# Attention and a two-layer FFN on one core: small vector operations with fewer SBUF operands, scale products on POOL, weights rebuilt through PSUM, and their scale from a Gram matrix

## The chip, the cores and the metric

The kernel runs on 1 core of one Trainium2 chip. The metric is the device time of one launch in microseconds (us); before the change its median is 1268.44 us over 3 runs (1267.27 to 1268.83). The core has five engines with their own instruction queues: PE multiplies matrices (its weight loads are listed as PEld), DVE is the vector engine, ACT the engine for activations, POOL the general-purpose engine, and SP only issues DMA transfers here. SBUF is the working memory, PSUM the memory that PE writes its products to; POOL has no operand in PSUM anywhere in this kernel.

## What is computed

Per batch and head (8 batches, 8 heads, 576 tokens, head dimension 64), attention drops every score that is more than tau (0.02) below its row's maximum:

```python
scores = scale * np.matmul(q, k.transpose(0, 1, 3, 2))
thresh = np.max(scores, axis=-1, keepdims=True) - tau
scores = np.where(scores >= thresh, scores, -1000000000.0)
attn = softmax(scores)
x = np.matmul(attn, v)
h = x @ w_in
g = np.where(h >= 1, h, np.where(h <= -1, 0.0, (h + 1) ** 2 / 4))
out = g @ w_out
```

The softmax has 1e-09 added to its denominator; x holds the heads side by side, 4608 tokens of 512; w_in is 512 x 2048 and w_out 2048 x 512. The q, k and v come in f32, laid out with the head dimension first; the two weights come in f64.

## The kernel before

**Numbers.** Every matrix product is made of f16 parts: an operand is scaled by a power of two, rounded to f16 (the high part), and the remainder is rounded to f16 again (the low part). A product of two such operands takes three matmuls or a doubled contraction. The power of two comes from the data: sums of squares are formed on PE (`sums`), and `pow2` (lines 226 to 228) turns them into scales with bit operations on DVE.

**Weights.** `add_w` treats each weight in 16 units of 128 x 512. The f64 words are loaded into a staging buffer as pairs of u32 (line 436; for w_in the place is the still unused part of the w_out tile `WO`, 8 slots; for w_out it is the ring `x`, 5 slots, which later holds the FFN's input). ACT rescales the upper words (line 444), and three DVE operations put the bits of an f32 together in `WI` or `WO` (lines 448, 452, 456: shift; or with the shifted lower word; or with the sign). Their first operand reads every second u32. ACT then squares the unit with an accumulator (line 460); one matmul with ones adds the 16 sums up (line 478), and a chain of small DVE operations (lines 482 to 488) makes the weight's scales `wsc`. Odd units are then normed on POOL (498), rounded on ACT (501), and their remainder is formed on POOL (504); even units are normed and rounded on ACT (511), with the remainder on DVE (514).

**q, k and v.** For each pair of heads (`add_qk`) ACT sums the squares of q and k into a tile `pc` of 40 columns, PE adds them up over partitions (301), DVE makes scales: `pow2` on 6 columns (226 to 228), a product with tau's constants (308), and two products of 3 columns (316, 317) for the softmax. POOL norms q and k (324), ACT rounds (327), POOL forms the remainder (331), and 8 DMAs lay the parts out in `qq` and `kk`. V is handled alike for each batch (`add_v`; remainder on DVE, 396; a DMA transpose into `vst`).

**Tiles.** A pair's 2 x 576 query rows make 9 tiles of 128 rows by 576 keys, 288 in all. In `add_tile` PE forms the scores (595) into one of two PSUM buffers; DVE takes the row maximum (606) and from it, with the pair's constants, the bias of exp and the threshold (607: two columns at once, from two SBUF operands and a scalar per partition); ACT takes exp (610); DVE applies the mask and sums (614) and forms the reciprocal (618, 619); POOL scales (622), ACT rounds (625), POOL forms the remainder (628), and a DMA transposes the two parts into `eT` (631). After the last tile of a half pair PE multiplies with V (668), ACT and DVE cut the result into the FFN's input `x` (676, 680).

**FFN.** For each 128 tokens and each 512 of the 2048 hidden columns: 48 matmuls (729), Relu and square on ACT (735, 738), the gate on DVE (742), f16 parts on ACT and DVE (746, 750), 12 matmuls into the only accumulator `acc` (756). After four such steps ACT scales the accumulator (785) and a DMA stores it.

**The order.** Nothing is scheduled by hand at the place where it is written. Each step is a `plan.op` with an engine, an assumed duration, a key (roughly the number of the tile at whose time it is due) and its dependencies; `Plan.order` plays the whole kernel through and writes down which step each engine starts next, the one with the lowest key among those that are ready and whose buffers are free. The instructions are then emitted in that order, and each engine keeps its own order on the chip whatever the real durations are. Keys: tile j has key j; w_in's unit u has 0.7u - 2, w_out's 12 + 0.7u; the FFN lags the tiles that feed it by `LEAD` = 8. PSUM has the pools `s` (2, scores), `ph` (3, everything else) and `acc` (1).

Of the kernel before, what the change touches and what calls it, by code (L numbers as in the profile page):

```python
# [32 lines left out]
class Op:  # L33
    def __init__(self, eng, cost, key, fn, work):
        self.eng, self.cost, self.key, self.fn, self.work = eng, cost, key, fn, work
        self.take, self.uses, self.next, self.behind, self.left = [], [], [], [], 0


class Plan:


    HOP, TO_PE, LAND = 0.25, 0.6, 2.2
# [29 lines left out]
    def order(self):  # L72
# [6 lines left out]
        now = 0.0  # L79
        while True:  # L80
            woke = False
            for e, q in ready.items():
                if not idle[e]:
                    continue
# [57 lines left out]
def attn_ffn_kernel(ctx: ExitStack, tc: tile.TileContext, qT, kT, vT, tau, w_in, w_out, out):  # L142
# [68 lines left out]
    wssq = {w: cp.tile([P, NU], F32, name=f"ssq_{w}") for w in WT}  # L211
# [19 lines left out]
    def consts():  # L231
# [47 lines left out]
    def add_qk(b, p, need):  # L279
# [12 lines left out]
        def ssq(buf, n):  # L292
            return lambda: A.activation(junk, ap(buf, raw), AF.Square, accum_out=ap(cb, pc)[:, n : n + 1])
# [11 lines left out]
        def scales():  # L305
            c = ap(cb, pc)
            pow2(stat(sb.slot, 6), c[:, 2:8], c[:, 8:14], c[:, 14:20])
            V.tensor_tensor(c[:, 20:22], c[:, 18:20], tcs[:, 0:2], ALU.mult)  # L308

        def scales2():  # L310
            c = ap(cb, pc)
            u = c[:, 8:14].rearrange("p (v t) -> p v t", t=2)
            x = c[:, 14:20].rearrange("p (v t) -> p v t", t=2)
            k1 = c[:, 24:30].rearrange("p (v t) -> p v t", t=2)
            k2 = c[:, 30:36].rearrange("p (v t) -> p v t", t=2)
            V.scalar_tensor_tensor(k1[:, :, 0], u[:, :, 0], 2.0 ** 102 * D ** -0.5, u[:, :, 1], ALU.mult, ALU.mult)
            V.scalar_tensor_tensor(k2[:, :, 1], x[:, :, 0], tcs[:, 2:3], x[:, :, 1], ALU.mult, ALU.mult)

        sc1 = plan.op("DVE", 0.6, key - 3, scales, [ps, t_op], uses=[cb, sb])
        sc2 = plan.op("DVE", 0.3, key - 2, scales2, [sc1], uses=[cb])  # L320
        done = []
        for n, (rb, nb, ld) in enumerate(((rq, nq, lq), (rk, nk, lk))):
            def norm(rb=rb, n=n):
                G.tensor_scalar(ap(rb, raw), ap(rb, raw), ap(cb, pc)[:, 20 + n : 21 + n], 1.0, ALU.mult, ALU.mult)  # L324
# [31 lines left out]
    def add_v(b, need):  # L356
# [17 lines left out]
        def sums():  # L374
            T.matmul(stat(sb.slot, NPAIR), ones, rows_bf16(vssq[:, b, :]), start=True, stop=True)
# [35 lines left out]
    def add_w(w, keys):  # L411
        stats, bits = [], []
        for u in range(NU):
            key = keys(u)
            sb = plan.buf("wst" if w == "i" else "x")
# [30 lines left out]
            def b1(stage=stage, dsu=dsu):  # L446
                if F64:
                    V.tensor_scalar(dsu, stage()[:, :, 1], 3, None, ALU.logical_shift_left)

            def b2(stage=stage, dsu=dsu):  # L450
                if F64:
                    V.scalar_tensor_tensor(dsu, stage()[:, :, 0], 29, dsu, ALU.logical_shift_right, ALU.bitwise_or)

            def b3(stage=stage, dsu=dsu):
                if F64:
                    V.scalar_tensor_tensor(dsu, stage()[:, :, 1], 1 << 31, dsu, ALU.bitwise_and, ALU.bitwise_or)
# [372 lines left out]
```

## Time and profile before

| | |
|---|---|
| median of 3 runs | 1268.44 us (1267.27 to 1268.83) |
| the profiled execution | 1266.92 us, of which the span from first to last instruction is 1265.0 us |
| mean granted PE clock | 0.958 |
| busy PE, DVE | 1079.4 us (85%), 1071.6 us (85%) |
| busy ACT, POOL | 891.7 us (70%), 801.6 us (63%) |
| DMA | 184.53 MB, mean 146 GB/s |

A row of the groups of instructions reads: line, engine, operation, what is written from what, shapes, count, then busy us and mean ns of one, then the idle time of the engine just before them and what ended it. A row of the timeline reads: start, length, engine, line, operation. An engine can start its next instruction slightly before the profile ends the last one, so the distance between two starts can be smaller than the length. A row of waits reads: who waited for whom, us in total, times, longest. Line numbers are those of the kernel before, unless it is said otherwise.

### The profile page before, as it was taken

To read this page: it belongs to the slowest core of one execution; us is meant where nothing else is said; L and a number is where in the kernel's file an instruction comes from. 1 tells how busy PE (TensorE), PEld (TensorE's weight loads), DVE (VectorE), ACT (ScalarE), POOL (GpSimd) and SP (SyncE) were. 2 spreads that over 40 slices of the span, in tenths; PEclk is the share of its full clock that TensorE was granted. 3 is DMA by queue.
4 is the path that set the end of the run, shared out by engine and by line. 5 is a ranking of instruction groups with operands and counts; after the bars stand their busy time and mean duration, and the time that the engine had idled before them with its cause. 6 is when DMAs were issued, how large, how long until landed. Compare 5 with 4: busy or idle time off the path is not lost.

```text
span 1265.0 us, 31411 instructions
## 1 busy us (share of the span) xinstructions
PE 1079.4 (85%) x11818; PEld 784.4 (62%) x11818; DVE 1071.6 (85%) x2613; ACT 891.7 (70%) x1558; POOL 801.6 (63%) x791
## 2 busy tenths in 40 slices
PE   0124388899889998999989988999989999999998
PEld 0112365576657766776657766677677776777675
DVE  6999999889887889988897999888897988988532
ACT  6676677686668777877676767867687767777544
POOL 3688488855685667666674667765685667655300
PEclk9966699899989999999999999999999999999999
DMA  9985746975698669965698568965788579755400
GB/s 318 295 196 121 166 87 131 209 140 116 132 203 177 104 108 184 209 129 109 132 204 157 104 108 194 201 127 103 157 200 162 92 124 179 149 104 99 78 10 18
DMA packets 443816, 184.53 MB, mean 146 GB/s; under 512 B 406288, under 2 KB 414480, under 8 KB 443664
## 3 DMA queue, kind: packets, MB, share of 16 engines
q1 hardware_dynamic: 443664, 182.52, 70.9%
q8 instruction: 93, 1.52, 0.5%
q14 instruction: 59, 0.48, 0.1%
HBM read 45.09 MB, written 9.44 MB: 43 GB/s over the span
## 4 chain that ended last, share of the span: by engine, by line
DVE 42%; PE 38%; ACT 6%; issue 6%; DMA 4%; POOL 3%; SPq 0%; ACTq 0%; DVEq 0%; POOLq 0%
PE acc L756 15%; PE ph L729 14%; DVE sm L606 9%; DVE sm L607 8%; DVE e L614 7%; PE s L595 5%; PE ph L668 4%; DVE ph L742 3%; DVE g L750 3%; ACT e L610 2%; DVE vb L396 2%; POOL e L622 1%; DMA WO<-in_moe_w_in_dram 1%; DVE sm L619 1%; DVE x L680 1%
## 5 line engine op out<-in xcount | busy, mean ns | idle before, releaser
L628 POOL TENSOR_TENSOR hl<-e,hl 128x576 f16<-128x576 f32 x288 | 372.2, 1297 | 115.0 <-ACT hl L625 110.1
L729 PE MATMUL ph<-x,WI 128*128 128x128 f16 x6912 | 413.4, 221 | 10.1 <-DVE x L680 6.7
L729 PEld LDWEIGHTS <-WI 128*128 128x128 f16 x6912 | 402.4, 99 | 26.9 <-issue 13.1
L756 PE MATMUL acc<-WO,g 128*128 128x512 f16 x1728 | 400.1, 381 | 13.3 <-DVE g L750 12.2
L622 POOL TENSOR_SCALAR e<-e,sm 128x576 f32<-128x576 f32 x288 | 226.5, 792 | 210.4 <-DVE sm L618 119.0
L610 ACT ACTIVATE e<-s,sm,pc 128x576 f32<-128x576 f32 x288 | 237.7, 828 | 153.6 <-DVE sm L607 109.6
L756 PEld LDWEIGHTS <-g 128*128 128x128 f16 x1728 | 164.6, 98 | 202.3 <-DVE g L750 20.1
L595 PE MATMUL s<-kk,qq 128*128 128x288 f16 (+1 forms) x1280 | 190.4, 300 | 97.8 <-DVE e L614 79.1
L625 ACT ACTIVATE hl<-e 128x576 f16<-128x576 f32 x288 | 194.6, 678 | 77.6 <-POOL e L622 76.2
L614 DVE SCALAR_TENSOR_TENSOR e<-s,sm,e 128x576 f32<-128x576 f32 x288 | 229.4, 810 | 21.0 <-ACT e L610 18.4
L606 DVE TENSOR_REDUCE sm<-s 128x1 f32<-128x576 f32 x288 | 215.2, 747 | 28.9 <-PE s L595 28.3
L595 PEld LDWEIGHTS <-qq 128*128 128x128 f16 (+1 forms) x1280 | 112.0, 103 | 163.7 <-issue 116.3
L607 DVE SCALAR_TENSOR_TENSOR sm<-pc,sm 128x2 f32<-128x2 f32 x288 | 166.2, 577 | 10.2
L742 DVE SCALAR_TENSOR_TENSOR ph<-ph,scs,asq 128x512 f32<-128x512 f32 (+1 forms) x160 | 111.6, 699 | 59.5 <-ACT asq L738 56.0
L735 ACT ACTIVATE asq<-ph,scs 128x512 f32<-128x512 f32 (+1 forms) x160 | 115.0, 730 | 43.2 <-PE ph L729 42.9
L668 PE MATMUL ph<-eT,vst 128*64 128x256 f16 (+1 forms) x1792 | 131.9, 302 | 6.6 <-DVE g L750 4.5
L750 DVE SCALAR_TENSOR_TENSOR g<-ph,scs,g 128x512 f16<-128x512 f32 (+1 forms) x160 | 108.6, 688 | 30.8 <-ACT g L746 30.8
L668 PEld LDWEIGHTS <-vst 128*64 128x64 f16 x1792 | 103.4, 116 | 36.5 <-issue 23.2
L746 ACT ACTIVATE g<-ph,scs 128x512 f16<-128x512 f32 (+1 forms) x160 | 100.4, 640 | 25.5 <-DVE ph L742 24.4
L331 POOL TENSOR_TENSOR nat<-raw,nat 128x576 f16<-128x576 f32 x64 | 85.4, 1338 | 15.6 <-ACT nat L327 15.2
L738 ACT ACTIVATE asq<-asq 128x512 f32<-128x512 f32 x144 | 90.1, 626 | 1.9
L324 POOL TENSOR_SCALAR raw<-raw,pc 128x576 f32<-128x576 f32 x64 | 48.1, 758 | 30.1 <-DVE pc L308 15.4
(99 smaller groups left out, 703.0 us busy)
## 6 DMA issues: line engine op xcount, KB each, us to landing
kk<-nat SPq DMA_DIRECT2D x128, 144.0 KB, 3.4
raw<-in_q_dram SPq DMA_DIRECT2D x32, 288.0 KB, 3.6
raw<-in_k_dram SPq DMA_DIRECT2D x32, 288.0 KB, 3.7
raw<-in_v_dram SPq DMA_DIRECT2D x32, 288.0 KB, 4.0
qq<-nat SPq DMA_DIRECT2D x128, 72.0 KB, 2.3
WO<-in_moe_w_in_dram SPq DMA_DIRECT2D x16, 512.0 KB, 8.1
x<-in_moe_w_out_dram SPq DMA_DIRECT2D x16, 512.0 KB, 4.3
out_dram<-o SPq DMA_DIRECT2D x32, 256.0 KB, 2.6
```

The lines of the kernel that those rows point to most:

```text
L595: T.matmul(ap(s, s_ps)[r, f, :SH], q[:, hd, c : c + n], k[:, hd, l, f * SH : (f + 1) * SH], start=l == 0, stop=l == 1)
L606: V.tensor_reduce(t[:, 0:1], sv(), AX.XY, ALU.max, negate=True)
L607: V.scalar_tensor_tensor(t[:, 1:3], c[:, 24 + 2 * v : 26 + 2 * v], t[:, 0:1], c[:, 30 + 2 * v : 32 + 2 * v], ALU.mult, ALU.add)
L610: A.activation(halves(ap(e, es)), sv(), AF.Exp, bias=ap(m, sm)[:, 1:2], scale=ap(cb, pc)[:, 24 + 2 * v : 25 + 2 * v])
L614: V.scalar_tensor_tensor(halves(ap(e, es)), sv(), t[:, 2:3], halves(ap(e, es)), ALU.is_ge, ALU.mult, accum_out=t[:, 3:4])
L622: G.tensor_scalar(ap(e, es), ap(e, es), ap(m, sm)[:, 5:6], 1.0, ALU.mult, ALU.mult)
L625: A.activation(ap(x, hl)[:, :S], ap(e, es), AF.Copy)
L628: G.tensor_tensor(ap(x, hl)[:, S:], ap(e, es), ap(x, hl)[:, :S], ALU.subtract)
L668: T.matmul(o[hd * D : (hd + 1) * D, :n], vt[:, k, hd * D : (hd + 1) * D], t[:, kb, hd * n : (hd + 1) * n], start=k == 0, stop=k == NVB - 1)
L729: T.matmul(h[:, i], WTh["i"][:, u, wl * 512 + c * P : wl * 512 + (c + 1) * P], x[:, cc, xl, c0 : c0 + P], start=m == 0, stop=m == 3 * NCC - 1)
L742: V.scalar_tensor_tensor(hv()[:, :, c], hv()[:, :, c], scs[:, b, 0:1], tv()[:, :, c], ALU.max, ALU.min)
L756: T.matmul(ap(ab, accs), gv()[:, i, gl], WTh["o"][:, fc + i, wl * 512 : (wl + 1) * 512], start=fc + i == 0 and m == 0, stop=fc + i == NFC ...
```

## The change

It has five parts.

1. *The tile's threshold*: the operation at line 607 becomes two operations of one column, each with one SBUF tensor, a scalar per partition and a constant. The two-column constants in `pc` become single columns; filling them with zeros and minus ones at the start is left out.
2. *The pair's scales*: `pc` holds every value in the first of two columns, so that `pow2` reads and writes with a stride of two; the three products (308, 316, 317) leave DVE and become five POOL operations, in two steps of the plan.
3. *The weights' bits*: the first two of the three DVE operations write a PSUM buffer of the pool `ph`, and the second and third read it back. The sum of squares on ACT goes. In its place PE multiplies each unit, taken as the upper halves of its f32 words (bf16), with its own transpose, and adds all units up in `acc`: a Gram matrix of 128 x 128, whose largest element in each row replaces the sum.
4. *The weights' split*: all units take the former odd units' way, with the norm on ACT in place of POOL and the remainder on POOL; none has its remainder on DVE.
5. *The order*: w_out is staged in two of the five slots of `x` until its last unit's bits are done; its keys become 10 + 0.5u; the first batch's V is due 4 tiles later; no fifth FFN step starts before w_out's last unit's bits; the planner lets SP issue nothing while more than 3 us of transfers are outstanding; several assumed durations change.

The core of the diff:

```diff
+                if e == "SP" and dma > now + self.QUEUE:
+                    if wake <= now:
+                        wake = dma - self.QUEUE + 1e-6
+                        heapq.heappush(events, (wake, -1, 3, e, None))
                     continue
...
+    plan.free["x"], plan.free["wso"] = [0, 1, 2], [3, 4]
-    pc = ring("pc", 6, [40], F32)
+    pc = ring("pc", 6, [36, 2], F32)
...
         def scales():
-            c = ap(cb, pc)
+            c = ap(cb, pc)[:, :, 0]
             pow2(stat(sb.slot, 6), c[:, 2:8], c[:, 8:14], c[:, 14:20])
-            V.tensor_tensor(c[:, 20:22], c[:, 18:20], tcs[:, 0:2], ALU.mult)
         def scales2():
+            c = ap(cb, pc)[:, :, 0]
+            G.tensor_tensor(c[:, 20:22], c[:, 18:20], tcs[:, 0:2], ALU.mult)
+        def scales3():
-            V.scalar_tensor_tensor(k1[:, :, 0], u[:, :, 0], 2.0 ** 102 * D ** -0.5, u[:, :, 1], ALU.mult, ALU.mult)
-            V.scalar_tensor_tensor(k2[:, :, 1], x[:, :, 0], tcs[:, 2:3], x[:, :, 1], ALU.mult, ALU.mult)
+            G.tensor_scalar(c[:, 24:27], u[:, :, 0], 2.0 ** 102 * D ** -0.5, 1.0, ALU.mult, ALU.mult)
+            G.tensor_scalar(c[:, 27:30], x[:, :, 0], tcs[:, 2:3], 1.0, ALU.mult, ALU.mult)
+            G.tensor_tensor(c[:, 24:27], c[:, 24:27], u[:, :, 1], ALU.mult)
+            G.tensor_tensor(c[:, 27:30], c[:, 27:30], x[:, :, 1], ALU.mult)
...
-                    V.tensor_scalar(dsu, stage()[:, :, 1], 3, None, ALU.logical_shift_left)
+                    V.tensor_scalar(ap(pb, ph).bitcast(U32), stage()[:, :, 1], 3, None, ALU.logical_shift_left)
-                    V.scalar_tensor_tensor(dsu, stage()[:, :, 0], 29, dsu, ALU.logical_shift_right, ALU.bitwise_or)
+                    t = ap(pb, ph).bitcast(U32)
+                    V.scalar_tensor_tensor(t, stage()[:, :, 0], 29, t, ALU.logical_shift_right, ALU.bitwise_or)
-                    V.scalar_tensor_tensor(dsu, stage()[:, :, 1], 1 << 31, dsu, ALU.bitwise_and, ALU.bitwise_or)
+                    V.scalar_tensor_tensor(dsu, stage()[:, :, 1], 1 << 31, ap(pb, ph).bitcast(U32), ALU.bitwise_and, ALU.bitwise_or)
...
-                A.activation(j, dst, AF.Square, accum_out=wssq[w][:, u : u + 1])
+            def gram(dst=dst, u=u):
+                t = cut(dst)
+                for x in range(4):
+                    c = t[:, x * P : (x + 1) * P]
+                    T.matmul(ap(gbuf, accs)[:, :P], c, c, start=u == 0 and x == 0, stop=u == NU - 1 and x == 3)
...
+        def largest():
+            V.tensor_reduce(wssq[w], ap(gbuf, accs)[:, :P], AX.X, ALU.max)
...
                 def norm(src=src):
-                    G.tensor_scalar(src, src, s[:, 0:1], 1.0, ALU.mult, ALU.mult)
+                    A.activation(src, src, AF.Copy, scale=s[:, 0:1])
...
     def w_pool(w, u):
-        return u % 2 == 1
+        return True
...
-        add_v(b, start[b, 0, 0])
+        add_v(b, start[b, 0, 0] + (0 if b else 4))
-    add_w("o", lambda u: 12 + 0.7 * u)
+    add_w("o", lambda u: 10 + 0.5 * u)
...
-            V.scalar_tensor_tensor(t[:, 1:3], c[:, 24 + 2 * v : 26 + 2 * v], t[:, 0:1], c[:, 30 + 2 * v : 32 + 2 * v], ALU.mult, ALU.add)
+            V.tensor_scalar(t[:, 1:2], t[:, 0:1], c[:, 24 + v, 0:1], None, ALU.mult)
+            V.tensor_scalar(t[:, 2:3], t[:, 0:1], -1.0, c[:, 27 + v, 0:1], ALU.mult, ALU.add)
...
+            nstep += 1
+            if nstep > len(gb):
+                wi.append(wbits["o", NU - 1])
```

More of the change, by code (lines that the diff above doesn't have):

```diff
@@ L125, in order @@
                     continue
+                if kind == 1 and o.gives:
+                    self.free[o.gives[0]] += o.gives[1]
                 for b in o.uses:
@@ L210, in attn_ffn_kernel @@
     tcs = cp.tile([P, 3], F32, name="tcs")
[L211 removed]
+    wssq = {w: cp.tile([P, 1], F32, name=f"ssq_{w}") for w in WT}
     wsc = {w: cp.tile([P, 8], F32, name=f"wsc_{w}") for w in WT}
@@ L462, in add_w @@
             before = []
             if w == "o":
-                before = [wssq_op["i", x] for x in range(NU) if wst["i", x] is not None and x % (NFC // 2) in ((u + 2) // 2,)]
+                before = [wbits["i", x] for x in range(NU) if x % (NFC // 2) == (u + 2) // 2]
             l = plan.op("SP", 0.6, key - 5, load, before, take=[sb], work=1.75)
-            o1 = plan.op("ACT", 0.67, key - 1, fix, [l], uses=[sb])
-            o2 = plan.op("DVE", 0.66, key, b1, [o1] + before, uses=[sb])
-            o3 = plan.op("DVE", 1.06, key, b2, [o2], uses=[sb])
@@ L469, in add_w @@
-            o4 = plan.op("DVE", 0.85, key, b3, [o3], uses=[sb])
-            o5 = plan.op("ACT", 0.75, key, ssq, [o4], uses=[sb])
-            wssq_op[w, u] = o5
-            stats.append(o5)
+            o1 = plan.op("ACT", 0.6, key - 1, fix, [l], uses=[sb])
+            o2 = plan.op("DVE", 0.55, key, b1, [o1] + before, take=[pb], uses=[sb])
+            o3 = plan.op("DVE", 0.62, key, b2, [o2], uses=[sb, pb])
+            o4 = wbits[w, u] = plan.op("DVE", 0.62, key, b3, [o3], uses=[sb, pb], behind=wbits.get((w, u - 1)))
@@ L473, in add_w @@
+            if not u:
+                gbuf = plan.buf("acc")
+            stats.append(plan.op("PE", 0.4, key, gram, [o4], take=[gbuf] if not u else [], uses=[gbuf], behind=stats[-1] if stats else None))
+        if w == "o":
+            o4.gives = ("x", [3, 4])
         sb = plan.buf("ph")
@@ L488, in scales @@
             V.tensor_scalar(s[:, 3:4], s[:, 4:5], 2.0 ** 89, None, ALU.mult)
-        ps = plan.op("PE", 0.1, key, sums, stats + [c_op], take=[sb])
+        lg = plan.op("DVE", 0.25, key, largest, stats, uses=[gbuf])
+        ps = plan.op("PE", 0.1, key, sums, [lg, c_op], take=[sb])
         so = wscale[w] = plan.op("DVE", 0.8, key, scales, [ps], uses=[sb])
@@ L633, in add_tile @@
         o = chained("qk", plan.op("PE", 0.5 if len(heads) == 1 else 0.7, j, qk, ready, take=[s], uses=[qb, kb], behind=prev.get("qk")))
-        o = chained("max", plan.op("DVE", 0.82, j, smax, [o, c2], take=[m], uses=[s, cb], behind=prev.get("max")))
+        o = chained("max", plan.op("DVE", 0.95, j, smax, [o, c2], take=[m], uses=[s, cb], behind=prev.get("max")))
         o = chained("exp", plan.op("ACT", 0.73, j, sexp, [o], take=[e], uses=[s, m, cb], behind=prev.get("exp")))
```

58 lines of the change are left out of this document (28 added, 30 removed).

## The prediction

> **What bounds the kernel now.** I read the page's busy times first, then a table of stretches, then PE's longest waits in the steady stretch.
>
> ```profile
> PE 1079.4 (85%) x11818; PEld 784.4 (62%) x11818; DVE 1071.6 (85%) x2613; ACT 891.7 (70%) x1558; POOL 801.6 (63%) x791
> ```
>
> ```profile
> 0.00:165.00 165.00, 50.15 (x354) 34.19 (x355) 149.79 (x336) 108.34 (x219) 105.04 (x109) 0.77 0.82 211
> 165.00:256.00 91.00, 75.43 (x774) 53.86 (x771) 83.24 (x185) 66.98 (x117) 76.16 (x73) 0.92 0.75 151
> 256.00:1100.00 844.00, 795.07 (x8926) 582.40 (x8925) 740.45 (x1873) 621.95 (x1070) 567.03 (x556) 0.99 0.77 149
> 1100.00:1200.00 100.00, 98.40 (x1108) 70.84 (x1106) 78.75 (x192) 66.72 (x107) 53.33 (x53) 1.00 0.52 95
> 1200.00:1265.00 65.00, 60.34 (x669) 43.11 (x665) 19.33 (x32) 27.70 (x47) 0.00 (x0) 1.00 0.05 14
> ```
>
> ```profile
> PE s L595 <- DVE e L614: 21.7, 25, 2.9
> ```
>
> PE and DVE tie over the span, but not at the same time. Columns of the table: stretch, length, busy PE, PEld, DVE, ACT, POOL, granted clock. Up to 165 us DVE is busy for 149.8 of 165 and PE for 50.2: the front is bound by DVE, which converts the weights and runs the first softmax tiles. From 256 to 1100 PE is busy for 795.1 of 844 (94.2%) beside a DVE at 740.5 (88%). PE's losses there lead to DVE: its greatest wait between 256 and 1200 us, 21.7 us in 25 times, is that of the scores for DVE's mask, which frees their buffer. From 1100 to 1200 DVE has fallen to 78.8%, and PE is at 98.4%. So in the steady stretch PE sets the pace and a late DVE takes some 5% from it; after 1200 only PE works, and this change does nothing there.
>
> Many small DVE instructions take far longer than their size.
>
> ```profile
> 106.46 1.27 POOL L628 TENSOR_TENSOR hl<-e,hl 128x576 f16<-128x576 f32 x1
> 106.59 1.17 DVE L607 SCALAR_TENSOR_TENSOR sm<-pc,sm 128x2 f32<-128x2 f32 x1
> ...
> 108.37 1.70 POOL L628 TENSOR_TENSOR hl<-e,hl 128x576 f16<-128x576 f32 x1
> ...
> 108.87 1.49 DVE L448 TENSOR_SCALAR WO<-x 128x512 uint32<-128x512 uint32 x1
> ...
> 121.21 0.22 DVE L607 SCALAR_TENSOR_TENSOR sm<-pc,sm 128x2 f32<-128x2 f32 x1
> 121.35 0.42 DVE L448 TENSOR_SCALAR WO<-x 128x512 uint32<-128x512 uint32 x1
> ```
>
> L607 works on two columns. It starts at 106.59, just behind a POOL instruction, and ends with it (107.76 against 107.73). With POOL idle it takes 0.22, and the next one starts 0.14 behind it. L448 shows the same: 0.42 free, 1.49 beside POOL. DVE waits for POOL within its instructions; a view of waits never shows it.
>
> **The change, part by part.**
>
> ```profile
> L607 DVE SCALAR_TENSOR_TENSOR sm<-pc,sm 128x2 f32<-128x2 f32 x288 | 166.2, 577 | 10.2
> L317 DVE SCALAR_TENSOR_TENSOR pc<-pc,tcs 128x3 f32<-128x3 f32 x32 | 14.9, 464 | 0.0
> L316 DVE SCALAR_TENSOR_TENSOR pc<-pc 128x3 f32<-128x3 f32 x32 | 11.6, 363 | 0.0
> L228 DVE TENSOR_SCALAR pc<-pc 128x6 uint32<-128x6 uint32 x32 | 14.7, 459 | 1.1
> L227 DVE TENSOR_SCALAR pc<-pc 128x6 uint32<-128x6 uint32 x32 | 13.3, 415 | 1.1
> L514 DVE SCALAR_TENSOR_TENSOR WO<-WO,wsc_o 128x512 f16<-128x512 f32 x8 | 9.5, 1191 | 0.0
> L514 DVE SCALAR_TENSOR_TENSOR WI<-WI,wsc_i 128x512 f16<-128x512 f32 x8 | 9.0, 1121 | 0.0
> ```
>
> ```profile
> 163.57 0.20 DVE L557 TENSOR_SCALAR scs<-scs,wsc_i 128x1 f32<-128x1 f32 x1
> 163.69 0.20 DVE L558 TENSOR_SCALAR scs<-scs,wsc_i 128x1 f32<-128x1 f32 x1
> ```
>
> *The tile's threshold.* L607 becomes two one-column operations with a pointer scalar, each with one SBUF tensor. L557 and L558 are such operations: they follow at 0.12, so two cost 0.24. L607 costs 0.577 less its overlap of 0.07, 0.50. DVE gains 0.25 a tile, 72 us over 288 tiles. Bounds: a gain of 0.15 (0.35 for the pair, if the first waits for the maximum) to 0.30.
>
> *The scales of a pair of heads.* L316, L317 and the product at L308 leave DVE, 26.5 us for the first two. POOL gets five small instructions a pair in their place. No row shows a POOL operation this small; none should exceed the 0.86 of L498 below, and I take 0.3: 32 x 5 x 0.3 = 48 us on an engine busy 63% of the span, hidden. They stand ahead of q and k's normalising and of the pair's first threshold, prepared two tiles ahead or more.
>
> L227 and L228 keep their form and get a stride of two columns. L448 above reads with a stride of two and waits for POOL all the same, so I give the stride nothing; if it did free them at 0.17, DVE would have 17 us less. The Trainium skill (VectorE: DVE Perf Modes, Mode 2×_2P — use both read ports for one tensor) asks for an SBUF source and destination and an even count for the two-port mode, and names no stride; by it too these two stay exposed, and the trace's L448 agrees.
>
> *The weights' bits.*
>
> ```profile
> L448 DVE TENSOR_SCALAR WI<-WO 128x512 uint32<-128x512 uint32 x16 | 8.5, 552 | 0.0
> L452 DVE SCALAR_TENSOR_TENSOR WI<-WO,WI 128x512 uint32<-128x512 uint32 x16 | 12.0, 765 | 0.0
> L456 DVE SCALAR_TENSOR_TENSOR WI<-WO,WI 128x512 uint32<-128x512 uint32 x16 | 12.7, 807 | 0.0
> L448 DVE TENSOR_SCALAR WO<-x 128x512 uint32<-128x512 uint32 x16 | 9.7, 613 | 1.5 <-ACT x L444 1.5
> L452 DVE SCALAR_TENSOR_TENSOR WO<-x,WO 128x512 uint32<-128x512 uint32 x16 | 12.5, 787 | 0.0
> L456 DVE SCALAR_TENSOR_TENSOR WO<-x,WO 128x512 uint32<-128x512 uint32 x16 | 15.6, 983 | 0.0
> ```
>
> ```profile
> 155.07 0.75 DVE L742 SCALAR_TENSOR_TENSOR ph<-ph,scs,asq 128x512 f32<-128x512 f32 x1
> 155.73 0.74 DVE L606 TENSOR_REDUCE sm<-s 128x1 f32<-128x576 f32 x1
> ```
>
> The six rows sum to 71.0; less 0.07 of overlap for each of 96, 64.3. L742, 512 columns with one operand in PSUM, holds DVE for 0.66. Three such for 32 units are 63.4. So the bits gain 1 us: what the blocked ones lose comes back, but the first of the three loses its 0.42. I count 1, with -3 to +8 for the range. The Trainium skill (VectorE: DVE Perf Modes, Why PSUM operands drop a tier) says that a PSUM operand rules out the two-port mode, so the first shift would take an element a cycle. An estimate by that page, 512 / 0.96 GHz = 0.53 plus the fixed part, is in line with L742.
>
> *The split of the weights.* L514 goes, 18.5 us of DVE. All 32 units take their norm on ACT and their remainder on POOL.
>
> ```profile
> L504 POOL TENSOR_TENSOR WO<-WO 128x512 f16<-128x512 f32 x8 | 10.6, 1321 | 3.7 <-ACT WO L501 3.7
> L498 POOL TENSOR_SCALAR WO<-WO,wsc_o 128x512 f32<-128x512 f32 x8 | 6.9, 859 | 1.9 <-DVE wsc_o L484 1.9
> ```
>
> For w_out POOL pays 16 x 1.3 = 21 in place of 17.5, and w_in is alike: 7 more in a front where POOL is busy 105 of 165. ACT trades its 32 squares against 32 norms and more splits of the same 512 columns: near nothing, on an engine busy 108 of 165.
>
> *The Gram matrix* is 128 matmuls of 128 columns on a PE that idles 115 us in the front. They sit in PE's order behind the third bit operation of their unit, with the next tile's scores behind them; the plan sets both orders alike. The matrix holds the only accumulator until w_out is summed; the second product needs w_out's scale anyway. I take 0, and up to 5 us for the wait.
>
> *The order.* Bits of w_out get keys 10 to 17.5 in place of 12 to 22.5, so five tiles move behind them. Its staging shrinks to two slots (a rival, below). The planner holds SP back while more than 3 us of transfers are outstanding.
>
> ```profile
> 34.22 7.65 DMA qq<-nat
> ```
>
> In the chain the second pair's q waits 7.65 behind bulk loads. Held back, they should let it pass: I take 4, from 0 to 8, and to -3 if a load comes late.
>
> **The sum.**
>
> ```profile
> 164.12 0.16 DVE L482 TENSOR_REDUCE wsc_o<-ph 128x1 f32<-128x16 f32 x1
> ...
> 173.05 1.24 PE L756 MATMUL acc<-WO,g 128*128 128x512 f16 x5
> ```
>
> ```profile
> L614 DVE SCALAR_TENSOR_TENSOR e<-s,sm,e 128x576 f32<-128x576 f32 x288 | 229.4, 810 | 21.0 <-ACT e L610 18.4
> L606 DVE TENSOR_REDUCE sm<-s 128x1 f32<-128x576 f32 x288 | 215.2, 747 | 28.9 <-PE s L595 28.3
> ```
>
> ```profile
> 0.00:165.00 165.00, 14.59 (x26) 0.77 0.82 211
> ```
>
> Front (the last row is L607 alone there): w_out's scale starts at 164.1 and the second product at 173.1. DVE loses 26 x 0.25 = 6.5 on thresholds, 9.0 on L514 for w_in, 3.3 on L316 and L317 (4 pairs x 0.83), 1 on bits, and the five moved tiles, at 0.81 + 0.75 + 0.25 each, 9: together 29, so the scale comes at about 135. The moved tiles' PE work is paid later: at most 5/26 of PE's 50 us, 10; much of that 50 ran at a low clock or was the first product, so 5. Net -24, with the 4 of the queue -28.
>
> From 165 to 256 DVE (83.2 of 91) loses w_out's 9.5, the pair products and a quarter microsecond a tile, over 15 in all, and is no longer the bound. At the 98.4% of the late stretch PE's 75.4 take 76.7, 14 less; for the clock at 0.92 I take 12.
>
> From 256 to 1100 DVE loses about 65 of its 740 (some 218 tiles x 0.25 and the pair products), 675 in a shorter 808, 84%. PE's 795.1 at 98.4% take 808: -36. It is a little optimistic, as 84% is more than 78.8%, and a little pessimistic, as the busy time of PE holds stalls too.
>
> -28 - 12 - 36 = -76. The profiled execution took 1266.92 (span 1265.0); the median is 1268.44, 1.5 above. 1266.9 - 76 + 1.5 = 1192, and I forecast **1190**.
>
> **Rivals.**
>
> - *The front doesn't move*: POOL, ACT or the loads take over from DVE there, and only the later parts gain: 1268 - 48 = 1220. For it: POOL takes 7 more. Against: POOL at 105 of 165 has room.
> - *The steady stretch doesn't gain*: the losses of PE are the rhythm of the chain through five engines, not DVE's load: 1268 - 28 - 12 = 1228. Against it stands the 98.4%.
> - *Two staging slots* (slower).
>
> ```profile
> 51.72 0.60 SPq L436 DMA_DIRECT2D x<-in_moe_w_out_dram  x1
> ```
>
> ```profile
> x<-in_moe_w_out_dram SPq DMA_DIRECT2D x16, 512.0 KB, 4.3
> ```
>
> Each of w_out's 16 units holds one of two slots from its load's issue to its last bit operation: 4.3 landing, the fix on ACT and three DVE operations, 0.7 + 2.0, and hops: about 8, so a unit each 4 us, 64 us. From about 50 us on, where the third of today's loads goes out, that ends at 115, ahead of 135. If DVE serves the three between tiles, a unit stays longer. At 13 us it is a unit each 6.5, 104 us; with gram, sums and scale behind it at 166, where it is now. The accumulator stays held and all of FFN waits. To eat the 48 of the later parts too, the scale must come after 212, which takes 19 us a slot: then 1270 and above, up to 1290. Against: the bits' low keys make DVE take them as soon as they land.
> - *The change doesn't do what it says*: if one-column operations still wait for POOL, two in place of one lose 0.1 to 0.5 a tile. Against: L557 and its neighbours run at 0.20, and no row of one column shows more.
>
> **How the numbers follow.** Forecast 0.68, front unmoved 0.11, steady unmoved 0.10, slots 0.07, one-column operations that wait 0.04. The forecast's own bounds: threshold 0.15 to 0.30, stride freed, bits +8, queue 8, and PE's stalls gone too, 1150 to 1215. The range 1150 to 1232 takes in both half cases; the two slower ones lie outside. A run of this kernel resolves about 0.2%. Faster by over 0.2%: 0.88; within: 0.03, where slots or waits just cancel the gain; slower: 0.09.
>
> **What would show it.** L607's successors at 0.2 or less each with no long ones among them; L227 and L228 still at 0.4 on average; w_out's scale near 135 us; PE busy over 97% between 256 and 1100; DVE's total near 950. Wrong if w_out's last bits come after 165, if PE still waits for the mask as long in the steady stretch, or if POOL is busy throughout the front.

## The result and the profile after

The changed kernel takes 1215.18 us (median of 4 runs, 1214.50 to 1219.17) against 1268.63 for the kernel before (4 runs, 1267.27 to 1269.32): a ratio of 0.9586 [0.9564, 0.9609], 53 us less. Below, the shares of engines in the chain of work that ended last, from the page of the kernel before and then of the changed kernel. After it come the changed kernel's table of stretches (columns as in the prediction) and PE's longest wait between 256 and 1200 us.

```profile
DVE 42%; PE 38%; ACT 6%; issue 6%; DMA 4%; POOL 3%; SPq 0%; ACTq 0%; DVEq 0%; POOLq 0%
```

```profile
PE 56%; DVE 19%; POOL 7%; ACT 7%; issue 5%; DMA 5%; SPq 1%; ACTq 0%; DVEq 0%; POOLq 0%
```

```profile
0.00:165.00 165.00, 75.78 (x691) 54.21 (x692) 139.40 (x382) 113.29 (x203) 111.66 (x143) 0.79 1.01 240
165.00:256.00 91.00, 80.92 (x815) 56.07 (x813) 67.73 (x190) 74.35 (x134) 75.08 (x81) 0.94 0.66 136
256.00:1100.00 844.00, 816.41 (x9228) 599.88 (x9227) 707.15 (x2108) 641.78 (x1100) 612.55 (x698) 0.99 0.79 152
```

```profile
PE s L619 <- DVE e L639: 10.8, 13, 4.2
```

PE's share of the chain that ended last has grown from 38% to 56%, and DVE's has fallen from 42% to 19%. Between 256 and 1100 PE is busy for 816.4 of 844 us, 96.7%, where it was 94.2%, and its wait for DVE's mask has halved, from 21.7 to 10.8 us. The granted clock of the first three stretches is nearly what it was: 0.79, 0.94 and 0.99 against 0.77, 0.92 and 0.99.

Busy time holds stalls, so the gain is better read from the count of matmuls behind PE's busy time in each stretch. By 256 us PE has started 691 + 815 = 1506 (a matmul that lies across a boundary is counted on both sides); 128 of them are the new Gram matmuls, which leaves 1378 against 354 + 774 = 1128 before. From 256 to 1100 it is 9228 against 8926. With 844 / 9228 = 0.0915 us for one, the 250 more by 256 us are worth 23 us, and the 302 more in the steady stretch 28. The sum, 51, is close to the gain of the profiled span (1265.0 to 1213.2, 51.8). An early matmul isn't quite the mean one, so the split is good to a few us. The same sum is made for the experiments below; I call it the matmul count.

The new threshold, by groups and in the timeline of the changed kernel:

```profile
L631 DVE TENSOR_SCALAR sm<-sm,pc 128x1 f32<-128x1 f32 x288 | 61.7, 214 | 10.4
L632 DVE TENSOR_SCALAR sm<-sm,pc 128x1 f32<-128x1 f32 x288 | 58.8, 204 | 0.0
```

```profile
22.11 0.21 DVE L631 TENSOR_SCALAR sm<-sm,pc 128x1 f32<-128x1 f32 x1
22.24 0.20 DVE L632 TENSOR_SCALAR sm<-sm,pc 128x1 f32<-128x1 f32 x1
22.36 0.15 DVE L394 TENSOR_REDUCE scs<-ph 128x1 f32<-128x4 f32 x1
```

The pair holds DVE from 22.11 to 22.36, 0.25 us. The shortest, the median and the longest of the 288 (the three figures behind the colon, in ns), first of L607 in the kernel before, then of the new pair:

```profile
L607 DVE SCALAR_TENSOR_TENSOR sm<-pc,sm x288: 220/502/3997, 29.0 to 1181.0; 128x2 f32<-128x2 f32 x144
```

```profile
L631 DVE TENSOR_SCALAR sm<-sm,pc x288: 212/214/217, 21.1 to 1128.7; 128x1 f32<-128x1 f32 x144
L632 DVE TENSOR_SCALAR sm<-sm,pc x288: 201/204/208, 21.2 to 1128.8; 128x1 f32<-128x1 f32 x144
```

Not one of the new operations is long. The old one took 0.577 us on average and 0.22 at its shortest, less than the pair. So the pair is no cheaper by itself; what it saves is the wait.

### The profile page after: what moved, and what is told of

Same layout as the page of the kernel before. It is cut to its first block, busy times and chain, and to the rows that moved or that the text cites. A ratio compares the mean times of both kernels' runs of the same rounds, so it can differ in the third digit from the quotient of the medians.

```text
span 1213.2 us, 31983 instructions
## 1 busy us (share of the span) xinstructions
PE 1081.5 (89%) x11946; PEld 788.4 (65%) x11946; DVE 961.9 (79%) x2789; ACT 885.1 (73%) x1526; POOL 819.6 (68%) x939
## 4 chain that ended last, share of the span: by engine, by line
PE 56%; DVE 19%; POOL 7%; ACT 7%; issue 5%; DMA 5%; SPq 1%; ACTq 0%; DVEq 0%; POOLq 0%
PE acc L781 22%; PE ph L754 21%; PE s L619 7%; PE ph L693 6%; DVE e L639 4%; DVE sm L630 4%; POOL hl L653 2%; POOL e L647 2%; DMA eT<-hl 2%; ACT e L635 1%; POOL nat L344 1%; DMA kk<-nat 1%; DVE ph L468 1%; DVE vb L409 1%; DVE ph L463 1%
## 5 line engine op out<-in xcount | busy, mean ns | idle before, releaser
L653 POOL TENSOR_TENSOR hl<-e,hl 128x576 f16<-128x576 f32 x288 | 368.0, 1283 | 98.8 <-ACT hl L650 96.4
L754 PE MATMUL ph<-x,WI 128*128 128x128 f16 x6912 | 409.3, 220 | 7.6 <-DVE x L705 4.6
L647 POOL TENSOR_SCALAR e<-e,sm 128x576 f32<-128x576 f32 x288 | 218.7, 765 | 163.1 <-DVE sm L643 86.0
L635 ACT ACTIVATE e<-s,sm,pc 128x576 f32<-128x576 f32 x288 | 236.4, 828 | 69.7 <-DVE sm L631 56.9
L619 PE MATMUL s<-kk,qq 128*128 128x288 f16 (+1 forms) x1280 | 187.7, 298 | 51.2 <-DVE e L639 45.1
L693 PE MATMUL ph<-eT,vst 128*64 128x256 f16 (+1 forms) x1792 | 127.8, 295 | 8.2 <-DVE g L775 4.0
L693 PEld LDWEIGHTS <-vst 128*64 128x64 f16 x1792 | 100.9, 113 | 32.5 <-issue 17.5
L344 POOL TENSOR_TENSOR nat<-raw,nat 128x576 f16<-128x576 f32 x64 | 81.6, 1280 | 8.7 <-ACT nat L340 8.2
L631 DVE TENSOR_SCALAR sm<-sm,pc 128x1 f32<-128x1 f32 x288 | 61.7, 214 | 10.4
L340 ACT ACTIVATE nat<-raw 128x576 f16<-128x576 f32 x64 | 43.2, 679 | 34.5 <-POOL raw L337 27.2
```

Source lines behind the costliest of these rows:

```text
L619: T.matmul(ap(s, s_ps)[r, f, :SH], q[:, hd, c : c + n], k[:, hd, l, f * SH : (f + 1) * SH], start=l == 0, stop=l == 1)
L635: A.activation(halves(ap(e, es)), sv(), AF.Exp, bias=ap(m, sm)[:, 1:2], scale=ap(cb, pc)[:, 24 + v, 0:1])
L647: G.tensor_scalar(ap(e, es), ap(e, es), ap(m, sm)[:, 5:6], 1.0, ALU.mult, ALU.mult)
L653: G.tensor_tensor(ap(x, hl)[:, S:], ap(e, es), ap(x, hl)[:, :S], ALU.subtract)
L693: T.matmul(o[hd * D : (hd + 1) * D, :n], vt[:, k, hd * D : (hd + 1) * D], t[:, kb, hd * n : (hd + 1) * n], start=k == 0, stop=k == NVB - 1)
L754: T.matmul(h[:, i], WTh["i"][:, u, wl * 512 + c * P : wl * 512 + (c + 1) * P], x[:, cc, xl, c0 : c0 + P], start=m == 0, stop=m == 3 * NCC - 1)
```

## The experiments

The theory: an operation of DVE with two SBUF operands waits for POOL inside the instruction; taking that wait out of the threshold, and work off DVE in the front, is what lets PE run closer to its limit. The rivals: the gain is the front's alone; or the hold-back on SP; or it is the planner's new order as such, since each edit changes durations and so the order of every step. No variant leaves out any part of the computation. The runs were made on several chips, each beside the kernel before on the same chip, so differences between two variants are taken from their ratios, times 1268.

### The threshold, alone and taken back

Two runs. The first is the kernel before with only the threshold's edit; the planner is told nothing of it, so every engine keeps the order of the kernel before:

```diff
-            V.scalar_tensor_tensor(t[:, 1:3], c[:, 24 + 2 * v : 26 + 2 * v], t[:, 0:1], c[:, 30 + 2 * v : 32 + 2 * v], ALU.mult, ALU.add)
+            V.tensor_scalar(t[:, 1:2], t[:, 0:1], c[:, 24 + 2 * v : 25 + 2 * v], None, ALU.mult)
+            V.tensor_scalar(t[:, 2:3], t[:, 0:1], -1.0, c[:, 31 + 2 * v : 32 + 2 * v], ALU.mult, ALU.add)
```

> The kernel before with one edit: the two-column threshold operation becomes two one-column operations; the order of all steps stays as it was. Theory (the gain comes from DVE no longer waiting for POOL inside small operations): DVE loses about 104 busy us in the profile (166 to 62 for two such operations, less 60 for the second: about 120 us in their place, so DVE near 1025), PE's busy share between 256 and 1100 us rises from 94.2% to about 96%, and the time falls by 20 to 30 us, to 1239 to 1249. Rival (the gain comes from the new order, with assumed durations nearer to the real ones): the time stays within 5 us of 1268.

Measured: 1237.45 us, 0.978 [0.9752, 0.9807], in the theory's range, with DVE at 1015.2 us of work. The second is the changed kernel with its old two-column operation put back, again in an unchanged order (12 small fills at the start are added):

```diff
+        for t in pc:
+            G.memset(t[:, 24:27, 1], -1.0)
+            G.memset(t[:, 29:32, 1], 0.0)
...
-            V.tensor_scalar(t[:, 1:2], t[:, 0:1], c[:, 24 + v, 0:1], None, ALU.mult)
-            V.tensor_scalar(t[:, 2:3], t[:, 0:1], -1.0, c[:, 27 + v, 0:1], ALU.mult, ALU.add)
+            f = c.rearrange("p n t -> p (n t)")
+            V.scalar_tensor_tensor(t[:, 1:3], c[:, 24 + v, :], t[:, 0:1], f[:, 59 + 2 * v : 61 + 2 * v], ALU.mult, ALU.add)
```

> The kernel after with the threshold formed by one two-column operation from two SBUF operands again, every engine's order being exactly that of the kernel after (the constants get a second column and 12 small fills at the start). Theory (the same operations in the same order differ only by the wait for POOL): the operation's mean is 0.5 to 0.6 us again and the time rises by 20 to 32 us, a ratio of 0.974 to 0.984 to before. Rival (the freed DVE time is no longer needed once the front and the order have changed): below 0.968.

Measured: 1244.19 us, 0.981 [0.9792, 0.9828]. The stretches from 0, 165 and 256 us, first of the threshold alone, then of the threshold taken back:

```profile
0.00:165.00 165.00, 51.73 (x389) 35.88 (x390) 148.04 (x366) 108.31 (x220) 105.59 (x110) 0.79 0.81 212
165.00:256.00 91.00, 78.63 (x804) 55.07 (x802) 80.32 (x215) 71.30 (x126) 78.61 (x76) 0.92 0.77 160
256.00:1100.00 844.00, 810.13 (x9159) 597.37 (x9158) 718.51 (x2147) 636.59 (x1094) 583.16 (x571) 0.99 0.78 151
```

```profile
0.00:165.00 165.00, 73.94 (x653) 52.23 (x654) 140.96 (x338) 109.32 (x196) 109.66 (x153) 0.77 0.94 235
165.00:256.00 91.00, 76.56 (x754) 53.81 (x752) 69.12 (x168) 72.93 (x130) 73.65 (x79) 0.92 0.68 135
256.00:1100.00 844.00, 800.18 (x9043) 587.75 (x9042) 732.08 (x1836) 628.77 (x1077) 602.24 (x686) 0.99 0.77 149
```

Threshold alone, by the matmul count: 65 more by 256 us (6 us) and 233 more in the steady stretch (22 us at 844 / 9159). Taken back from the changed kernel: 99 fewer (9 us) and 185 fewer (17 us). So from both sides, with the order of every engine fixed, it is worth 28 us (1 - 0.978 and 0.981 - 0.9586, each 0.022, times 1268), most of it in the steady stretch. Without the threshold the other parts still have 0.981, and on top of it they have 0.9586 / 0.978 = 0.980: the two halves add up.

Where it acts, in groups of the kernel with the threshold taken back, then of the changed kernel (ACT's exp, with its idle time and the releasers, is the last row of each):

```profile
L635 DVE SCALAR_TENSOR_TENSOR sm<-pc,sm 128x2 f32<-128x2 f32 x288 | 163.4, 567 | 10.3
L638 ACT ACTIVATE e<-s,sm,pc 128x576 f32<-128x576 f32 x288 | 237.8, 829 | 133.0 <-DVE sm L635 88.9 <-DVE sm L646 31.8 <-PE ph L505 2.2
```

```profile
L635 ACT ACTIVATE e<-s,sm,pc 128x576 f32<-128x576 f32 x288 | 236.4, 828 | 69.7 <-DVE sm L631 56.9 <-DVE sm L632 10.9 <-PE ph L309 0.8
```

The operation is 0.567 again, and ACT idles 133.0 us ahead of exp in place of 69.7. Of the 63 us between them, 21 are waits for the threshold itself (88.9 against 56.9 + 10.9). Another 32 are put down to L646, the step before the reciprocal, which is not among the releasers in the changed kernel's row; why it is here isn't shown. The threshold stands between the row maximum and exp of every tile, so a delay there reaches exp, the mask and the scores' buffer after it: PE's wait for the mask between 256 and 1200 us is 17.6 us with the old operation and 10.8 without. DVE's busy total differs too (1015.1 against 961.9 us), and the runs don't separate the delay in the chain from the load on DVE.

### Freeing DVE elsewhere: the pair products

The kernel before with the products of a pair's scales on POOL:

```diff
-            V.tensor_tensor(c[:, 20:22], c[:, 18:20], tcs[:, 0:2], ALU.mult)
+            G.tensor_tensor(c[:, 20:22], c[:, 18:20], tcs[:, 0:2], ALU.mult)
...
-            V.scalar_tensor_tensor(k1[:, :, 0], u[:, :, 0], 2.0 ** 102 * D ** -0.5, u[:, :, 1], ALU.mult, ALU.mult)
-            V.scalar_tensor_tensor(k2[:, :, 1], x[:, :, 0], tcs[:, 2:3], x[:, :, 1], ALU.mult, ALU.mult)
+            G.tensor_scalar(k1[:, :, 0], u[:, :, 0], 2.0 ** 102 * D ** -0.5, 1.0, ALU.mult, ALU.mult)
+            G.tensor_scalar(k2[:, :, 1], x[:, :, 0], tcs[:, 2:3], 1.0, ALU.mult, ALU.mult)
+            G.tensor_tensor(k1[:, :, 0], k1[:, :, 0], u[:, :, 1], ALU.mult)
+            G.tensor_tensor(k2[:, :, 1], k2[:, :, 1], x[:, :, 1], ALU.mult)
```

> The kernel before with the pair's three small products moved from DVE to five POOL operations, pc not strided. Theory: DVE loses 33 busy us, POOL gains about 40; only a part of that lies where PE waits for DVE, so the time falls by 4 to 12 us, to 1256 to 1264. Rival (the order decides): within 3 us of 1268. A loss would mean that POOL's queue delays q and k.

Measured: 1276.56 us, 1.009 [1.0064, 1.0115], slower by 11, as neither the theory nor the rival had it. Its busy times, and the first product among its groups:

```profile
PE 1082.0 (85%) x11818; PEld 785.9 (62%) x11818; DVE 1038.0 (82%) x2517; ACT 891.1 (70%) x1558; POOL 838.0 (66%) x951
```

```profile
L311 POOL TENSOR_TENSOR pc<-pc,tcs 128x2 f32<-128x2 f32 x32 | 10.7, 333 | 33.3 <-DVE pc L228 25.1 <-DVE sm L624 7.0
```

DVE has lost 33.6 us of work (1071.6 to 1038.0) and the kernel has become slower: DVE's total alone doesn't set the time. POOL now stands idle for 33.3 us in front of the product, 25.1 of them for the scales that DVE makes, and what is queued behind it on POOL waits as well. That this idle time is what costs the 11 us is likely but not shown, as the edit also moves the order. Then the other way about: the changed kernel with these products back on DVE, the strided layout kept.

```diff
-            G.tensor_tensor(c[:, 20:22], c[:, 18:20], tcs[:, 0:2], ALU.mult)
+            V.tensor_tensor(c[:, 20:22], c[:, 18:20], tcs[:, 0:2], ALU.mult)
...
-            G.tensor_scalar(c[:, 24:27], u[:, :, 0], 2.0 ** 102 * D ** -0.5, 1.0, ALU.mult, ALU.mult)
-            G.tensor_scalar(c[:, 27:30], x[:, :, 0], tcs[:, 2:3], 1.0, ALU.mult, ALU.mult)
-            G.tensor_tensor(c[:, 24:27], c[:, 24:27], u[:, :, 1], ALU.mult)
-            G.tensor_tensor(c[:, 27:30], c[:, 27:30], x[:, :, 1], ALU.mult)
+            V.scalar_tensor_tensor(c[:, 24:27], u[:, :, 0], 2.0 ** 102 * D ** -0.5, u[:, :, 1], ALU.mult, ALU.mult)
+            V.scalar_tensor_tensor(c[:, 27:30], x[:, :, 0], tcs[:, 2:3], x[:, :, 1], ALU.mult, ALU.mult)
```

> The kernel after with the pair's three products back on DVE (pc stays strided). Theory (from the run that moved them alone and lost 11 us: POOL waits for DVE ahead of them, with its whole queue behind): faster than the kernel after by 3 to 12 us, 1203 to 1212, although DVE has some 25 us more. Rival (DVE's load decides): slower by 3 to 10 us, 1218 to 1225.

Measured: 1228.64 us, 0.9698 [0.9661, 0.9735], also slower, by 14 against the changed kernel, where the theory had it faster by 3 to 12. The two answers contradict each other if the products have one effect of their own: alone their move costs 11 us, and undone in the changed kernel it costs 14. Both edits also make the planner choose another order; the runs on the order, below, show what that alone can do.

### The front: a third staging slot, and the split of the weights

The changed kernel with three slots for w_out in place of two:

```diff
-    plan.free["x"], plan.free["wso"] = [0, 1, 2], [3, 4]
+    plan.free["x"], plan.free["wso"] = [0, 1], [2, 3, 4]
...
-    o4.gives = ("x", [3, 4])
+    o4.gives = ("x", [2, 3, 4])
```

> The kernel after with three of the ring's five buffers for staging w_out in place of two. Theory (two slots pace w_out's conversion, 6.9 us a unit): the last bits come at about 140 in place of 158 us, w_out's scale at about 143 in place of 161, and the time falls by 5 to 15 us, to 1200 to 1210. Rival (the front is bound by the transfers or by DVE's own work): the scale stays within 5 us of 161 and the time within 3 us of 1215. Second rival (the scale comes earlier, but the FFN's input has one buffer less meanwhile): scale earlier, time unchanged.

Measured: 1226.61 us, 0.9698 [0.9667, 0.9729], slower than the changed kernel by 14, which none of the three answers had. In the timeline of the changed kernel, the third and the last of w_out's 16 loads, w_out's scale and the first second product:

```profile
65.69 0.37 SPq L449 DMA_DIRECT2D x<-in_moe_w_out_dram  x1
...
143.97 0.59 SPq L449 DMA_DIRECT2D x<-in_moe_w_out_dram  x1
...
162.89 0.16 DVE L237 TENSOR_SCALAR wsc_o<-ph 128x1 f32<-128x1 f32 x1
...
177.41 2.75 PE L781 MATMUL acc<-WO,g 128*128 128x512 f16 x12
```

The same three steps with three slots:

```profile
125.30 0.55 SPq L449 DMA_DIRECT2D x<-in_moe_w_out_dram  x1
...
144.03 0.15 DVE L237 TENSOR_SCALAR wsc_o<-ph 128x1 f32<-128x1 f32 x1
...
153.19 2.75 PE L781 MATMUL acc<-WO,g 128*128 128x512 f16 x12
```

Two slots do pace the front: 13 loads in 143.97 - 65.69 = 78.3 us are 6.0 a unit, 12 us a slot. A third brings the scale 19 us forward, and the second product 24. It isn't worth anything in the end: its stretches up to 1100 us give

```profile
0.00:165.00 165.00, 81.41 (x718) 57.81 (x719) 139.63 (x379) 115.87 (x207) 112.73 (x139) 0.79 0.93 228
165.00:256.00 91.00, 78.55 (x809) 55.29 (x807) 70.63 (x191) 71.64 (x128) 71.97 (x83) 0.94 0.81 155
256.00:1100.00 844.00, 806.09 (x9085) 589.49 (x9083) 699.81 (x2090) 635.44 (x1091) 610.19 (x695) 0.99 0.77 151
```

21 matmuls more by 256 us (2 us), but 143 fewer after it (13 us); the two profiled spans differ by 10.5. The earlier second product only exchanges one kind of PE work for another: by 256 us PE has run 145 matmuls of it against 144 in the changed kernel, 48 more of the first product and 28 fewer of the product with V. The loss lies behind 256 us, where the order planned after it differs.

The changed kernel with the split of every second unit as before (the even units' remainder on DVE):

```diff
     def w_pool(w, u):
-        return True
+        return u % 2 == 1
```

> The kernel after with the split of the weights shared out as before: the remainders of even units on DVE, those of odd units on POOL with the norm on ACT. Theory (DVE's load counts): DVE has about 18 us more and waits for POOL in them; the time rises by 3 to 10 us, to 1218 to 1225. Rival (POOL is the tighter engine in the front after the change): the time falls by 2 to 8 us.

Measured: 1225.20 us, 0.9688 [0.9666, 0.9710], 13 us slower; by its table of stretches 63 fewer matmuls by 256 us (6 us) and 52 fewer in the steady stretch (5 us). The first figure is where the edit acts, but the order differs there too; the second lies after all weights are done, where only the order differs.

### The order as such, and the hold-back

The same instructions of the changed kernel, in the order that the planner writes when it assumes 0.30 or 0.20 us for a hop between engines in place of 0.25:

```diff
-HOP, TO_PE, LAND, QUEUE = 0.25, 0.6, 2.2, 3.0
+HOP, TO_PE, LAND, QUEUE = 0.30, 0.6, 2.2, 3.0
```

> The kernel after, with one number of the planner changed: its assumed delay between engines 0.30 in place of 0.25 us. Every instruction is the same, only their order on the engines differs. Theory that grew out of the run with three slots (the order alone is worth about 10 us in the steady stretch): the time lies 4 to 15 us from 1215, in either direction. Rival (the loads of the engines decide, the order is noise): within 3 us of 1215.

> The same with 0.20 us: another draw of the order with the same instructions. Theory (order): 4 to 15 us from 1215 in either direction; together with the run with 0.30 this gives a rough width of what the order is worth. Rival: within 3 us of 1215.

Measured: 1228.28 us, 0.9688 [0.9674, 0.9703], with 0.30, and 1216.33 us, 0.959 [0.9572, 0.9608], with 0.20. One reordering costs 13 us, the other nothing. The same was done to the kernel before:

> The kernel before with the planner's assumed delay at 0.30 in place of 0.25 us: the same instructions in another order. Theory (the order is a draw worth some 10 us for any such kernel): 3 to 15 us from 1268 in either direction, more likely slower. Rival (the kernel before is bound by DVE and the order matters less to it): within 3 us.

> The same with 0.20 us: a second other order of the kernel before. Theory: 3 to 15 us from 1268 in either direction. Rival: within 3 us.

Measured: 1266.96 us, 0.9987 [0.9975, 0.9998], and 1269.63 us, 1.0014 [1.0003, 1.0025]: there the order moves the time by 2 us. The hold-back of SP, added to the kernel before with the new threshold (planner only):

```diff
+                if e == "SP" and dma > now + self.QUEUE:
+                    if wake <= now:
+                        wake = dma - self.QUEUE + 1e-6
+                        heapq.heappush(events, (wake, -1, 3, e, None))
+                    continue
```

> The kernel before with two edits: the threshold as two one-column operations, and the planner's hold-back of SP at 3 us of outstanding transfers. Against the threshold alone (ratio 0.978 to before, about 1240 on the first chip). Theory (hold-back moves only the first scores, and the rest of the gain needs the weights' and the split's part): 0 to 8 us less, a ratio of 0.972 to 0.978. Rival (the order of the transfers is what the remaining 25 us come from): a ratio of 0.965 or less.

Measured: 1242.73 us, 0.9801 [0.9786, 0.9816], beside 0.978 [0.9752, 0.9807] without it: no gain from the hold-back in that kernel.

What follows: in the changed kernel an order that is different but no more sensible on paper costs up to 13 us. The results there with one part taken back or altered and a new order (13, 14 and 14 us) are about as large, so none of them is shown as an effect of its part. The 11 us of the products alone belong to the kernel before, where the two other orders moved the time by 2 us each; they are more than that, but two orders are few. The threshold was measured with the order held, and so is the last experiment, below.

### The stride, and a version that frees these operations

In the changed kernel the two 6-column operations still wait for POOL. Below are its groups, then L238 in the timeline away from a POOL operation, L238 beside one, and that POOL operation:

```profile
L238 DVE TENSOR_SCALAR pc<-pc 128x6 uint32<-128x6 uint32 x32 | 17.5, 545 | 1.1
L239 DVE TENSOR_SCALAR pc<-pc 128x6 uint32<-128x6 uint32 x32 | 17.1, 534 | 1.1
```

```profile
50.19 0.17 DVE L238 TENSOR_SCALAR pc<-pc 128x6 uint32<-128x6 uint32 x1
```

```profile
72.67 0.81 DVE L238 TENSOR_SCALAR pc<-pc 128x6 uint32<-128x6 uint32 x1
```

```profile
72.29 1.16 POOL L528 TENSOR_TENSOR WI<-WI 128x512 f16<-128x512 f32 x1 [1.43 <-ACT WI L525]
```

The blocked one ends at 73.48 and POOL's operation at 73.45. The last experiment leaves the values of the pair in PSUM until the last step, in the order of the changed kernel:

```diff
-            pow2(stat(sb.slot, 6), c[:, 2:8], c[:, 8:14], c[:, 14:20])
+            o = stat(sb.slot, 6)
+            V.tensor_scalar(o, o, 2.0 ** -60, None, ALU.max)
+            V.tensor_scalar(o.bitcast(U32), o.bitcast(U32), 1, EXPM, ALU.logical_shift_right, ALU.bitwise_and)
+            V.tensor_scalar(c[:, 8:14].bitcast(U32), o.bitcast(U32), EXPM, None, ALU.bitwise_and)
+            V.tensor_scalar(c[:, 14:20].bitcast(U32), o.bitcast(U32), EXPM, None, ALU.bitwise_xor)
```

> The kernel after with the pair's power-of-two scales formed in PSUM: four DVE operations with at most one operand in SBUF, in place of three of which two read and write SBUF with a stride of two; same order on every engine. Theory (the stride does not keep them from waiting for POOL, PSUM does): the two long groups of 0.54 us become 0.15 to 0.2 each, DVE loses 20 to 25 busy us, and the time falls by 3 to 10 us, a ratio of 0.951 to 0.956. Rival (they lie beside PE's work or are replaced by the next wait): within 3 us of the kernel after, 0.957 to 0.961.

Measured: 1210.17 us (5 runs), 0.9543 [0.9528, 0.9557], 5 us less than the changed kernel, and an interval that lies below that kernel's [0.9564, 0.9609]. Its groups:

```profile
L318 DVE TENSOR_SCALAR pc<-ph 128x6 uint32<-128x6 uint32 x32 | 5.3, 165 | 1.1
L319 DVE TENSOR_SCALAR pc<-ph 128x6 uint32<-128x6 uint32 x32 | 4.9, 154 | 0.0
```

One operand in PSUM takes them from 0.54 to 0.16, although there is one operation more. DVE's busy total falls by 14.7 us (961.9 to 947.2). The forecast was 20 to 25. The two long groups alone lose 24.4 (34.6 to 10.2), but the operation that is added takes 5.5 (L317 there), and the remainder of V on DVE, which the edit leaves alone, takes 6.5 more than it did (37.2 to 43.7): a part of the wait has moved on, as the rival had it. This version beats both kernels.

## Why the prediction was right in its direction and too large

**PE as the bound, a late DVE as its loss: right.** The steady stretch gained where the prediction put it, with the mask's wait halved and PE's share up. No run speaks for "the steady stretch doesn't gain". That rival's mechanism is not out, though: the threshold is both work on DVE and a step of the tile's chain, and its removal would help either way.

**The threshold at 0.24 a pair: right.** The pair takes 0.25 and no long ones are left (the longest took 0.217). "One-column operations that wait" is out. The prediction counted its 72 us as DVE's time; in time of the kernel it was 28, the largest single piece, and the only part of the change shown by itself.

**The stride gives nothing: right**, and by the last experiment the 17 us that it left on the table were there: 14.7 us of DVE and 5 us of time. The forecast of 0.4 on average was low, 0.54. The Trainium skill (VectorE: DVE Perf Modes, Mode 2×_2P — use both read ports for one tensor) asks for SBUF on both sides and names no stride; the trace agrees, with 0.54 strided in SBUF against 0.16 from PSUM.

**The bits through PSUM at about nothing: right in size.** In the groups of the changed kernel:

```profile
L463 DVE TENSOR_SCALAR ph<-x 128x512 uint32<-128x512 uint32 x16 | 11.1, 691 | 5.4 <-ACT x L457 5.3
L468 DVE SCALAR_TENSOR_TENSOR ph<-x,ph 128x512 uint32<-128x512 uint32 x16 | 11.0, 686 | 0.1
L472 DVE SCALAR_TENSOR_TENSOR WO<-x,ph 128x512 uint32<-128x512 uint32 x16 | 10.9, 681 | 0.2
```

With w_in's three they are 65.7 us against 71.0. Whether the Gram matrix costs anything was not tried by itself. PE idles 42.6 us in front of its matmuls, 37.2 of them for the third bit operation, in a front where it idles 89 us in all; the prediction allowed up to 5 us for that wait.

**POOL's prices: right, a little high.** The five products, in the changed kernel's groups:

```profile
L320 POOL TENSOR_TENSOR pc<-pc,tcs 128x2 f32<-128x2 f32 x32 | 10.7, 335 | 17.7 <-DVE sm L643 8.6 <-DVE pc L239 7.7 <-DVE scs L579 0.3
L327 POOL TENSOR_SCALAR pc<-pc,tcs 128x3 f32<-128x3 f32 x32 | 8.6, 268 | 2.9
L326 POOL TENSOR_SCALAR pc<-pc 128x3 f32<-128x3 f32 x32 | 6.8, 214 | 2.4
L329 POOL TENSOR_TENSOR pc<-pc 128x3 f32<-128x3 f32 x32 | 6.8, 213 | 0.0
L328 POOL TENSOR_TENSOR pc<-pc 128x3 f32<-128x3 f32 x32 | 6.3, 198 | 0.0
```

They sum to 39.2 us against the 48 assumed. What the prediction left out is the idle time in front of the first one, 17.7 us here and 33.3 where the move was made alone: it called the step hidden because POOL has room, and didn't ask what an engine with a fixed order does while it waits for the operand. What that idle time costs the kernel isn't shown.

**The front: the step that failed.** The prediction put w_out's scale "at about 135" and took 28 us from that, and 12 from the stretch behind it. The scale came at 162.89, where it was before (164.12). The cause is what the prediction listed as the rival "two staging slots": 12 us a slot (it wrote 13), a unit each 6.0 us, and a scale "at 166". But that rival's price fell too: it let all of FFN wait behind the scale, while PE had 250 matmuls more done by 256 us, worth 23 us, with the second product even later than before (177.41 against 173.05). PE had other products to do, the first product of the FFN above all. Up to 165 us, in the kernel before and in the changed one:

```profile
L729 PE MATMUL ph<-x,WI 128*128 128x128 f16 x79 | 6.3, 255 | 0.0
```

```profile
L754 PE MATMUL ph<-x,WI 128*128 128x128 f16 x265 | 18.2, 235 | 3.0 <-DVE x L705 1.7 <-DVE g L775 1.3
```

By 256 us the 250 more are 144 of the first product, 56 of the product with V, 28 of the second product and 22 of the scores. So the front's gain came, but not by the path of the prediction, which had it come through an earlier scale of w_out; that this term has the right sign is in part luck. By 165 us every variant of the changed kernel has run 192 to 288 of the first product's matmuls, and every variant of the kernel before 48 to 114, the threshold alone among them; which part of the change lets them go earlier isn't shown. So 23 in place of 40, of which the threshold has 6 by itself. The other 17 belong to the remaining parts together: the pair's scales, the split, the bits, the Gram matrix and their order. They were not separated further; the split's share was 6 in the one run on it, within what an order can do. The hold-back's 4 us are not confirmed.

**The steady stretch: a term mis-sized.** 36 us, from PE at the 98.4% of the late stretch; it reached 96.7%, where the prediction's sign asked for over 97%, and by the matmul count 28 us. The prediction named the reason why 98.4% might be optimistic (DVE at 84% there, against 78.8% late). DVE was at 83.8% there, which fits, though no run shows it to be the cause. The prediction's 65 us less for DVE in this stretch come to 75 by its own terms (218 x 0.25 and 24 pairs x 0.83), so its 84% should have been 82%; the 36 don't hang on it. The threshold alone brings 22 of the 28.

**DVE's total near 950**: 961.9. Some 7 of the 12 us between are L238 and L239, 34.6 us against 28.0 of L227 and L228.

What stays open: about 25 us, the part of the gain that isn't the threshold. It is there with the old threshold (0.981) and with the new (a further 0.980), so it is real for this set of parts in this order. In the other orders and variants with the new threshold (0.9543 to 0.9698) it is 10 us at the least, by the ratios. Which of the parts brings it the runs don't say, since every edit made here that takes one of them back moves the order too, and an order alone moves 13 us. Taking each back with the order written out and held was not tried.

## What to carry to other kernels

Compare a small vector operation's mean duration with its size: 0.58 us for two columns is a wait inside the instruction, which no view of waits lists, and here it cost most where it stands in the chain of every tile, between the maximum and exp. Don't book an engine's freed microseconds as time of the kernel: here an edit that took 33.6 us off DVE went with a slower kernel, and one that took 14.7 us off it with one 5 us faster. Where a planner writes the order, compare an edit with the order held, or over several orders, before believing ten microseconds.

## What the runs showed that was not expected

- The changed kernel looks more sensitive to its order than the kernel before, by two other orders of each: the same change of one planner constant moves it by 13 us in one direction and not at all in the other (0.9590 against 0.9586), and the kernel before by 2 each way. Why was not found.
- The 6-column operations of the scales took 0.54 on average in the changed kernel and 0.44 before. With the products back on DVE and the stride kept, the second of them had a mean of 0.341 where it now has 0.534, so the stride is not what makes them longer. L238 took 0.17 away from a POOL operation and 0.81 beside one, so what they cost seems to depend on what POOL does at that time.
- A second product that starts 24 us earlier, with three slots, was worth nothing: by 256 us PE had run 145 of its matmuls against 144.
